# Attention and gated MLP, two layers, one token: output projection with the weights moving, and a new order of loads

## The chip, the cores and the metric

The kernel runs on one core of a Trainium2 chip. The metric is the time of one execution on the device in microseconds. Five runs of the kernel before gave 333.4 to 336.81, median 335.89.

## The reference

Four sequences (B), one new token each, model width 512. An attention block has 32 query heads of width 128 in 8 groups (four heads share one key and value head) and a cache of 4096 positions. Then comes a gated MLP of width 1792. Both blocks are applied twice, with the same weights and the same caches:

```
def _A_ref(x, k_cache, v_cache, wq, wo):
    q = (x @ wq).reshape(B, Sq, Hq, Dh) ...
    k = jnp.repeat(k_cache, rep, axis=1)
    v = jnp.repeat(v_cache, rep, axis=1)
    scores = jnp.einsum("bhqd,bhkd->bhqk", q, k) * (Dh ** -0.5)
    p = _softmax(scores, axis=-1)
    o = jnp.einsum("bhqk,bhkd->bhqd", p, v)
    return ... @ wo

def _B_ref(x, w_gate, w_up, w_down):
    h = _sigmoid(x @ w_gate) * (x @ w_up)
    return h @ w_down

x = x + _A_ref(_layernorm(x), k_cache, v_cache, wq, wo)
x = x + _B_ref(_layernorm(x), w_gate, w_up, w_down)
x = x + _A_ref(_layernorm(x), k_cache, v_cache, wq, wo)
x = x + _B_ref(_layernorm(x), w_gate, w_up, w_down)
```

Keys and values of a batch are each 8 groups x 4096 x 128 in bf16, 8 MiB; for four batches 32 MiB of keys and 32 MiB of values. They do not fit on the chip beside the weights, and layer 1 needs them again.

## The kernel before

**Tiles and slots.** A group's keys or values of one batch, 1 MiB, are loaded as two pieces of 512 KB (q = 0 and 1). A ring of 22 slots of one piece each (`NS`, `ring`) holds them; the weights have buffers of their own. Every load is issued by SyncE (SP), in the order that the string `order` spells (L413): a digit is a quarter of wq, a to d a quarter of wo, g, u, w the three MLP weights, k two K pieces (two groups, one q), V a V tile for layer 0, v a V tile for layer 1, r the K pieces of a batch that are loaded again. A load waits until the slot that it is given has no readers left. SP takes its queue strictly in order, so a load that waits for a slot holds up all loads behind it.

**What stays and what is loaded again.** V is loaded twice, once for each layer. K of a batch is loaded once, and its 16 pieces stay in the ring from layer 0's scores to layer 1's, but for those that `again` lists for the batch (L363, repeated at L414): these give their slot up after layer 0 and are loaded again by r.

**Work on one batch, layer 0.** VectorE transposes each K piece in place (`transpose_k`, L564). TensorE forms scores of a half of the groups (s = 0 or 1) in a bank S_ps, with q spread over a block-diagonal tile qbd as the stationary side and K moving, 16 matmuls of 512 columns for each q, each in a strip of 32 rows of the bank (`scores`, L577). `softmax` takes the maximum on VectorE, exponentials on ScalarE, and turns the probabilities with TensorE through the bank PT_ps into pt_sb. `values` multiplies V by them: narrow (L711), with V stationary, 32 matmuls of 4 columns for a group, or wide (`wide`, L673), with V moving, eight matmuls of 256 columns for a piece into the bank W_ps, which ScalarE copies into a bf16 high part (w_hi) and VectorE into a low part (w_lo), folded into O_ps by eight short matmuls. The tuple `NARROW` says which groups are narrow: in layer 0 all are, as in layer 1 those used before layer 0 of the next batch and those of the last batch; the other tiles of layer 1 are wide. VectorE scales O_ps into oT (L720). `y_proj` multiplies oT by wo: for each head four matmuls with wo stationary (128 x 128) and one column (four in layer 1) moving, all added up in the bank Y_ps over the 32 heads.

**From layer 0 to layer 1 (`cross`).** When the last V tile of a batch is used, `add_y` adds y to x, `glu` multiplies by wg and wu, `norm` makes the statistics (its matmuls go to the bank PT_ps), `centre` corrects for the mean on VectorE, `down` multiplies by wd, and `add_y` again gives layer 1's input. `q_proj` multiplies it by wq, `q_spread` makes qbd on TensorE and VectorE (L547), and layer 1's scores follow. Only when they are done do slots with K pieces come free. The last batch's layer 1 ends in `last_cross`, for all four batches at once.

**Order of instructions.** Nothing is ordered by hand within an engine. Each operation is put down with a duration, a priority (smaller is more urgent; steps of the cross have 0 or PX = 0), what it reads and writes; `_Sched.place` then plays the whole kernel through with these durations, a rate for the loads, a start-up charge after a pause (`RAMP`), and a time between blocks of TensorE's instructions (`FETCH`, `BLOCK`). Whenever an engine is free it takes, among the operations that could start within 0.05 us of the first, the most urgent. The order found so is written out, one in-order queue for each engine.

Of the kernel before, what the change touches and what calls it, by code (L numbers as in the profile page):

```python
# [6 lines left out]
ACTF = mybir.ActivationFunctionType  # L7
# [8 lines left out]
RAMP = 0.3  # L16
BLOCK = 256
FETCH = 5.7
PAIR = 0.0268
DRAIN = 0.13  # L20
# [21 lines left out]
class _Sched:  # L42
    def __init__(self, nslots):
        self.all = []
        self.last_write = {}
        self.readers = {}
        self.nslots = nslots
        self.bus = []

# [41 lines left out]
    def place(self):  # L91
# [18 lines left out]
        begun, crossed = 0, -FETCH  # L110
# [18 lines left out]
        while True:  # L129
            best = None  # L130
            for e in ENGINES:
# [3 lines left out]
                o = min((o for o in pending[e] if max(free_at[e], o.est) <= first + 0.05), key=lambda o: (o.prio, o.seq))  # L135
                t = max(free_at[e], o.est)
# [82 lines left out]
def bass_interleave_layers__gqa_block_cached__glu_gated_glu__decode_kernel(nc, A_x, A_k, A_v, A_wq, A_wo, B_x, B_wg, B_wu, B_wd, out):  # L219
# [22 lines left out]
    S = _Sched(NS)  # L242
    es = ExitStack()
# [66 lines left out]
    sel_o = sb("sel_o", [P, 2 * R], bf)  # L310

# [41 lines left out]
    S.put("pool", lambda e: e.memset(sel_o[:], 0.0), 0.1, 0, writes=["sel_o", "pl"])  # L353
    for a in range(4):
        S.put("pool", affine(sel_o, sel_o[:], [[-1, 2 * R]], -32 * a, 1.0), 0.2, 0, reads=["sel_o"], writes=["sel_o", "pl"])
    for name, t, v in (("ml0", ml, 1.0), ("S0", S_ps[0], 0.0), ("S1", S_ps[1], 0.0), ("S2", S_ps[2], 0.0), ("W", W_ps, 0.0)):
        S.put("dve", lambda e, t=t, v=v: e.memset(t[:], v), 0.4, 0, writes=[name])
# [5 lines left out]
    again = (((3, 1),), ((6, 1), (7, 0), (7, 1)), ((6, 1), (7, 1)), ((6, 0), (6, 1), (7, 0), (7, 1)))  # L363
# [49 lines left out]
    order = 'k10bkkkkk3Vk2VVkdVVcVagVVuwrvkkkkkkVvkkVVVVVVVvvkvvvkrkkkkvkvvVkVVVVVVVvvkvvvrkkkvvkvkkkVVVVVVVVrvvvvvvvvvvvvvv'  # L413
    again = (((3, 1),), ((6, 1), (7, 0), (7, 1)), ((6, 1), (7, 1)), ((6, 0), (6, 1), (7, 0), (7, 1)))  # L414
# [63 lines left out]
    def add_y(b, y, scal, skey, res, rkey, mi, prio):  # L478
# [4 lines left out]
            ), 0.2, prio, reads=["Y", rkey] + skey, writes=["xT"],  # L483
# [4 lines left out]
            ), 0.3, prio, reads=["Y", rkey] + skey, writes=["xj", "xsum0"],  # L488
# [45 lines left out]
    PS0, PS1, PL0, PL1, PV0, PV1, PK0, PK1, PDEN, PEV = (1.77, 1.93, -0.4, 1.55, 2.05, 1.65, 2.13, 2.82, 2.29, 1.1)  # L534
    cnt = {"u": 0}
    pt_free = list(range(NPT))
# [126 lines left out]
    def wide(l, b, s, pi, prio, gis):  # L663

        n = len(gis)
        for i, gi in enumerate(gis):
            for q in range(2):
                tile = V[l, b, 4 * s + gi, q]
                fns = []
                for j in range(HT // 2):  # L670
                    def fn(e, i=i, gi=gi, q=q, j=j, tile=tile):
                        a, t = j % 4, q * HT + 2 * j
                        return e.matmul(  # L673
                            W_ps[32 * a:32 * a + 2 * R, i * 256:i * 256 + 256],
# [5 lines left out]
                S.put("pe", fns, WIDE + DRAIN, prio, reads=[f"pt{pi}"], writes=["W"], tiles=[tile])  # L680
        w = 256 * n
        S.put(
            "act", lambda e: e.activation(w_hi[:, 0:w], W_ps[:, 0:w], ACTF.Copy), 0.62 if n > 1 else 0.4, PEV, reads=["W"],
# [3 lines left out]
            "dve", lambda e: e.tensor_tensor(w_lo[:, 0:w], W_ps[:, 0:w], w_hi[:, 0:w], ALU.subtract),  # L687
            0.65 if n > 1 else 0.4, PEV, reads=["W", "w_hi"], writes=["w_lo"],
# [10 lines left out]

    def values(l, b, s, pi, prio, gis, narrow):  # L700

        ws = [gi for gi in gis if gi not in narrow]
        for i in range(0, len(ws), 2):
            wide(l, b, s, pi, prio, ws[i:i + 2])
# [19 lines left out]
    def y_proj(l, s, prio, gis=range(4)):  # L724
        nb = 1 if l == 0 else B
        for gi in gis:
            fns = []
            for h in range(16 * s + gi * R, 16 * s + gi * R + R):
                for j in range(KD):
                    r = oT1[:, h:h + 1] if l == 0 else oT2[:, h, :]  # L730
                    fns.append(mm(
                        Y_ps[:, 0:nb * KD].rearrange("p (b k) -> p b k", b=nb)[:, :, j], wo[:, h, j * P:(j + 1) * P], r,
                        h == 0 and j == 0, h == H - 1 and j == KD - 1,
                    ))
# [236 lines left out]
```

## Time and profile before

| | |
|---|---|
| profiled execution, its own time | 335.89 us |
| its span, first to last instruction | 334.0 us |
| DMA, loads of SP: bytes, share of 16 engines | 119.82 MB, 93.9% |
| mean rate over the span | 361 GB/s |
| PE busy, matmuls | 208.6 us, 4968 |
| VectorE busy | 164.7 us |
| transposes of K pieces (L564) | 74, mean 1229 ns, 89.9 us |
| loads of K pieces / V pieces | 74 / 128, 512 KB each |
| projection by wo (Y_ps), layer 0 / layer 1 | 512 / 128 matmuls, mean 165 / 168 ns |
| copy of 512 columns to w_hi / subtraction to w_lo | mean 591 / 688 ns |

Busy times of matmuls overlap, so their mean is not the distance between two of them. Shares are means over the whole span; which resource ends last differs from stretch to stretch, so stretches are read apart. In the rows of stretches, the columns are: from and to in us, length, busy time (and count) of PE, its weight loads, VectorE, ScalarE, GpSimd, then the clock granted to TensorE, the share of the DMA engines, and GB/s. In rows of a timeline: start and duration in us, engine, line, operation, output <- inputs, shapes, and in brackets how long the engine idled before it and what ended that. The times at which single pieces land are the last of the 16 completions that the trace has for each load.

### The profile page before, as it was taken

What the parts mean: (1) busy time and instruction counts of PE and PEld (TensorE: products, weight loads), DVE (VectorE), ACT (ScalarE), POOL (GpSimd) and SP (SyncE); (2) the same over time, 40 slices, a digit from 0 to 9 for tenths busy, and PEclk for the clock granted to TensorE, in tenths of its full rate; (3) what the DMA queues carried; (4) which work ended last, traced back from release to release, by engine and by line L of the source; (5) the groups of instructions that cost most, each with busy time, mean ns of one, the idle gap of its engine ahead of it and who ended that gap; (6) DMA issues with size and microseconds to landing.
All of it is one profiled execution on the core that took longest, in us unless ns stands there. A gap on an engine that the chain in (4) does not pass through costs nothing.

```text
span 334.0 us, 11181 instructions
## 1 busy us (share of the span) xinstructions
PE 208.6 (62%) x4968; PEld 143.3 (43%) x4968; DVE 164.7 (49%) x418; ACT 62.3 (19%) x145; POOL 27.9 (8%) x111
## 2 busy tenths in 40 slices
PE   0224355444468677576865686868585766799864
PEld 0201323344433246454422455654142556565763
DVE  7088332002399781054996730348879404564013
ACT  1102013000014233000244221002154110105100
POOL 5201001000001111000000110000111000001101
PEclk9999999999995565555756555557555555567555
DMA  6999999999949999999999999987999999999930
GB/s 222 384 410 400 402 386 387 386 407 371 369 135 374 413 407 365 412 407 363 291 392 413 408 400 398 410 352 234 404 413 406 410 408 404 401 331 396 411 147 3
DMA packets 38337, 120.54 MB, mean 361 GB/s; under 512 B 3472, under 2 KB 9360, under 8 KB 38288
## 3 DMA queue, kind: packets, MB, share of 16 engines
q1 hardware_dynamic: 38256, 119.82, 93.9%
q8 instruction: 39, 0.64, 0.8%
q14 instruction: 10, 0.08, 0.1%
q10 hardware_dynamic: 32, 0.00, 0.0%
HBM read 119.80 MB, written 0.00 MB: 359 GB/s over the span
## 4 chain that ended last, share of the span: by engine, by line
DMA 50%; PE 18%; SPq 10%; issue 9%; DVE 8%; ACT 3%; POOLq 0%; POOL 0%; ACTq 0%; DVEq 0%
DMA ring<-in_A_v_cache_dram 32%; DMA ring<-in_A_k_cache_dram 18%; SPq L369 8%; PE S_ps L577 6%; DVE ring L564 3%; PE M_ps L326 3%; PE Y_ps L326 3%; PE W_ps L673 3%; PE O_ps L711 2%; ACT p_sb L618 2%; DVE ml L594 2%; SPq L390 2%; PE PT_ps L326 1%; ACT qbd L553 1%; DVE tr L611 0%
## 5 line engine op out<-in xcount | busy, mean ns | idle before, releaser
L564 DVE STREAM_TRANSPOSE ring<-ring 128x1024 int32<-128x1024 int32 x74 | 89.9, 1229 | 28.9 <-DMA ring<-in_A_k_cache_dram 28.4
L711 PE MATMUL O_ps<-pt_sb,ring 128*128 128x4 bf16 x1472 | 50.9, 167 | 34.4 <-DMA ring<-in_A_v_cache_dram 31.6
L577 PE MATMUL S_ps<-ring,qbd 128*16 128x512 bf16 x512 | 57.1, 598 | 19.6 <-DVE ring L564 12.3
L711 PEld LDWEIGHTS O_ps<-pt_sb,ring 128*128 128x128 bf16 x1472 | 45.4, 104 | 45.3 <-DMA ring<-in_A_v_cache_dram 32.6
L618 ACT ACTIVATE p_sb<-S_ps,cols 128x512 bf16<-128x512 f32 x32 | 24.6, 772 | 85.8 <-DVE cols L613 65.6
L577 PEld LDWEIGHTS S_ps<-ring,qbd 128*16 128x16 bf16 x512 | 14.2, 116 | 43.2 <-issue 25.1
L720 DVE TENSOR_TENSOR oT<-O_ps,winv 128x8 bf16<-128x8 f32 (+2 forms) x16 | 2.7, 166 | 59.3 <-PE O_ps L711 59.2
L594 DVE TENSOR_REDUCE ml<-S_ps 128x1 f32<-128x512 f32 x32 | 21.4, 668 | 13.2 <-PE S_ps L577 13.2
L673 PE MATMUL W_ps<-ring,pt_sb 128*8 128x256 bf16 x288 | 18.0, 381 | 8.5 <-DMA ring<-in_A_v_cache_dram 8.5
L326 PE MATMUL Y_ps<-oT,wo 128*128 128x1 bf16 x512 | 17.2, 165 | 6.4 <-DVE oT L720 3.6
L326 PEld LDWEIGHTS Y_ps<-oT,wo 128*128 128x128 bf16 x512 | 15.5, 104 | 7.9 <-DVE oT L720 4.4
L326 PE MATMUL PT_ps<-ident_b,p_sb 128*128 128x64 bf16 x128 | 12.4, 237 | 9.9 <-ACT p_sb L618 9.9
L326 PE MATMUL M_ps<-xT,wq 128*128 128x1 bf16 (+1 forms) x512 | 14.9, 164 | 4.7 <-issue 3.6
L326 PEld LDWEIGHTS M_ps<-xT,wq 128*128 128x128 bf16 x512 | 14.0, 100 | 8.2 <-issue 5.9
L460 POOL TENSOR_TENSOR cols<-cols 128x1 f32<-128x1 f32 (+1 forms) x10 | 6.6, 656 | 126.8 <-DVE cols L456 105.2
L643 POOL TENSOR_TENSOR cols<-cols 128x1 f32<-128x1 f32 x16 | 3.1, 193 | 158.8 <-ACT p_sb L618 158.8
L326 PEld LDWEIGHTS PT_ps<-ident_b,p_sb 128*128 128x128 bf16 x128 | 7.5, 119 | 17.4 <-ACT p_sb L618 13.8
L326 PE MATMUL Y_ps<-p_sb,wd 128*128 128x1 bf16 (+1 forms) x280 | 8.4, 166 | 10.3 <-DVE p_sb L754 6.3
L774 ACT ACTIVATE p_sb<-p_sb,cols 128x14 f32<-128x14 f32 x4 | 1.2, 307 | 68.1 <-DVE p_sb L518 47.1
L638 ACT ACTIVATE pt_sb<-PT_ps 128x512 bf16<-128x512 f32 x16 | 9.5, 596 | 20.6 <-PE PT_ps L326 20.6
L626 ACT ACTIVATE p_sb<-PT_ps 128x512 bf16<-128x512 f32 x16 | 9.5, 596 | 20.2 <-PE PT_ps L326 17.8
L326 PEld LDWEIGHTS Y_ps<-p_sb,wd 128*128 128x128 bf16 x280 | 7.9, 104 | 11.9 <-DVE p_sb L754 7.8
(118 smaller groups left out, 205.5 us busy)
## 6 DMA issues: line engine op xcount, KB each, us to landing
ring<-in_A_v_cache_dram SPq DMA_DIRECT2D x128, 512.0 KB, 10.8
ring<-in_A_k_cache_dram SPq DMA_DIRECT2D x74, 512.0 KB, 11.1
wq<-in_A_wq_dram SPq DMA_DIRECT2D x4, 1024.0 KB, 12.5
wo<-in_A_wo_dram SPq DMA_DIRECT2D x4, 1024.0 KB, 12.7
wg<-in_B_w_gate_dram SPq DMA_DIRECT2D x1, 1792.0 KB, 15.6
wu<-in_B_w_up_dram SPq DMA_DIRECT2D x1, 1792.0 KB, 17.2
wd<-in_B_w_down_dram SPq DMA_DIRECT2D x1, 1792.0 KB, 21.9
w_hi<-in_A_x_dram SPq DMA_DIRECT2D x1, 4.0 KB, 1.7
```

The lines of the kernel that those rows point to most:

```text
L326: return lambda e: e.matmul(o, lhsT=l, rhs=r, start=start, stop=stop)
L369: return e.dma_start(ring[t.slot], t.src.rearrange("(p t) d -> p (t d)", p=P)[:, q * TS:(q + 1) * TS])
L390: S.put("sp", lambda e: e.dma_start(o, i), 0.43, 0, writes=[key], dma=key, nbytes=nbytes, rate=rate)
L460: "pool", lambda e: e.tensor_tensor(rs, vpe[:, 0:nb], mhalf[:, 0:nb], ALU.pow), 0.6, prio,
L564: return e.transpose(v, v)
L577: return e.matmul(bank[32 * gi:32 * gi + 16, :], lhsT=qbd[u % NQB][:, gi, nn, :], rhs=kt[:, :, nn // 2, :, nn % 2], start=nn == 0, stop=nn ...
L594: "dve", lambda e, q=q: e.tensor_reduce(ml[:, q:q + 1], S_ps[banks[q]][:], AX.X, ALU.max, negate=True), 0.65,
L618: "act", lambda e, q=q: e.activation(p_sb[:, 4 * q:4 * q + 4, :].rearrange("p c x -> p (c x)"), S_ps[banks[q]][:], ACTF.Exp, bias=nbias, s ...
L626: "act", lambda e: e.activation(pt1.rearrange("p c g a h -> p (c g a h)"), PT_ps[:], ACTF.Copy), 0.65, prio,
L638: "act", lambda e: e.activation(pt_sb[pi][:].rearrange("p c g t h -> p (c g t h)"), PT_ps[:], ACTF.Copy), 0.65,
L673: return e.matmul(W_ps[32 * a:32 * a + 2 * R, i * 256:i * 256 + 256], lhsT=pt_sb[pi][:, t // 4, gi, t % 4:t % 4 + 2, :].rearrange("p t h - ...
L711: return e.matmul(O_ps[:, gi * R:(gi + 1) * R], lhsT=ring[tile.slot][:, (t % HT) * DH:(t % HT + 1) * DH], rhs=pt_sb[pi][:, t // 4, gi, t % ...
```

## The change

`y_proj` has wo as the moving side for groups 0 to 6: each of the four heads of a group takes a strip of 32 rows of Y_ps (one row used, four in layer 1), with oT as the stationary side and 512 columns of wo moving; the strips add up over the groups. After group 6 the bank is split into a high and a low part (w_hi by ScalarE, w_lo by VectorE), and eight matmuls with the new selector `sel_y` sum the strips and turn them into columns in PT_ps. Group 7, the last tile, is added there the old way. y, the up product of `glu` and `down` therefore live in PT_ps, no longer in Y_ps, and the statistics move to whichever scores bank is idle (`spare`). `wide` takes its bank as an argument. Group ranges in which layer 0 uses V follow `parts` (three groups, then one, for both halves). The planner gets new constants and a `look`: on VectorE an urgent operation that becomes ready within 0.7 us is preferred to one that could start now. The order of loads and the list of reloads are new; K pieces loaded again go from 1, 3, 2, 4 to 1, 0, 0, 3 for batches 0 to 3.

```diff
-RAMP = 0.3
+RAMP = 0.4
-FETCH = 5.7
+FETCH = 6.1
...
-        begun, crossed = 0, -FETCH
+        begun, crossed = 63, -FETCH
...
                 o = min((o for o in pending[e] if max(free_at[e], o.est) <= first + 0.05), key=lambda o: (o.prio, o.seq))
+                near = [
+                    p for p in pending[e]
+                    if p.prio <= 0 < o.prio and max(free_at[e], p.est) <= first + min(self.look.get(e, 0.0), o.dur)
+                ]
+                if near:
+                    o = min(near, key=lambda p: (p.est, p.seq))
...
+    S.look = dict(zip(("dve", "pe", "act"), (0.7, 0.0, 0.0)))
...
+    sel_y = sb("sel_y", [P, B], bf)
...
-    again = (((3, 1),), ((6, 1), (7, 0), (7, 1)), ((6, 1), (7, 1)), ((6, 0), (6, 1), (7, 0), (7, 1)))
+    again = (((7, 1),), (), (), ((5, 1), (6, 1), (7, 1)))
...
-    order = 'k10bkkkkk3Vk2VVkdVVcVagVVuwrvkkkkkkVvkkVVVVVVVvvkvvvkrkkkkvkvvVkVVVVVVVvvkvvvrkkkvvkvkkkVVVVVVVVrvvvvvvvvvvvvvv'
+    order = 'bk1kkk0dkV2kVkV3kVVVcVagVuwrvkkkkkvkkvkVvVVVVVVVvkvkvkrkvkkvvkkVVVVVVVVvvvrvkkkkkvkvkvvkVVVVVVVVvvvvvvrvvvvvvvv'
...
-    PS0, PS1, PL0, PL1, PV0, PV1, PK0, PK1, PDEN, PEV = (1.77, 1.93, -0.4, 1.55, 2.05, 1.65, 2.13, 2.82, 2.29, 1.1)
+    PS0, PS1, PL0, PL1, PV0, PV1, PK0, PK1, PDEN, PEV = (1.77, 2.41, -0.4, 1.76, 2.04, 1.65, 1.02, 2.04, 0.59, 1.1)
...
+    def spare():
+
+        i = (2 * cnt["u"] + 2) % 3
+        return S_ps[i], f"S{i}"
...
-    def y_proj(l, s, prio, gis=range(4)):
+    def y_proj(l, s, prio, gis):
...
+            if g < G - 1:
+                fns = [
+                    mm(Y_ps[32 * a:32 * a + nb, :], of(g * R + a), wo[:, g * R + a, :], g == 0, g == G - 2) for a in range(R)
+                ]
+                S.put("pe", fns, 0.43 + DRAIN, prio, reads=keys, writes=["Y"])
+            else:
+                fns = []
+                for h in range(g * R, g * R + R):
+                    for j in range(KD):
+                        fns.append(mm(y[:, :, j], wo[:, h, j * P:(j + 1) * P], of(h), False, h == H - 1 and j == KD - 1))
+                S.put("pe", fns, 0, prio, reads=keys, writes=["PT"])
+            if g == G - 2:
+                S.put("act", lambda e: e.activation(w_hi[:], Y_ps[:], ACTF.Copy), 0.62, prio, reads=["Y"], writes=["w_hi"])
+                S.put(
+                    "dve", lambda e: e.tensor_tensor(w_lo[:], Y_ps[:], w_hi[:], ALU.subtract), 0.65, prio,
+                    reads=["Y", "w_hi"], writes=["w_lo"],
+                )
+                fns = []
                 for j in range(KD):
+                    for x, half in enumerate((w_hi, w_lo)):
+                        fns.append(mm(y[:, :, j], half[:, j * P:(j + 1) * P], sel_y[:, 0:nb], j == 0 and x == 0, False))
+                S.put("pe", fns, 0, prio, reads=["w_hi", "w_lo", "sel_y"], writes=["PT"])
...
-        g, u = glu(n, lambda k: xT[:, k, 0:n], "xT", lambda: norm(b, 0, 4.0, rs, "rs_h", PT_ps, "PT", prio), prio)
+        g, u = glu(n, lambda k: xT[:, k, 0:n], "xT", lambda: norm(b, 0, 4.0, rs, "rs_h", *spare(), prio), prio)
...
+    def parts(narrow):
+
+        if len(narrow) == 4:
+            return range(0, 3), range(3, 4)
+        if 3 in narrow:
+            return range(0, 2), range(2, 3), range(3, 4)
+        return range(0, 2), range(2, 4)
```

## The prediction

> **What bounds the kernel now.** I read the page's slices first, then busy time by stretches, then the chain that ended last in order of time, then the timeline of VectorE in one stretch.
>
> ```profile
> span 334.0 us, 11181 instructions
> PE 208.6 (62%) x4968; PEld 143.3 (43%) x4968; DVE 164.7 (49%) x418; ACT 62.3 (19%) x145; POOL 27.9 (8%) x111
> ...
> DMA  6999999999949999999999999987999999999930
> ...
> q1 hardware_dynamic: 38256, 119.82, 93.9%
> q8 instruction: 39, 0.64, 0.8%
> ```
>
> No engine is near full; the loads are. Where the DMA row shows less than 9 there are a start, a tail, and holes in between: one for each batch, when layer 1's queries of that batch are being made (I call these turns 0 to 3). In stretches (the last two columns are DMA share and GB/s):
>
> ```profile
> 88.00:92.00 4.00, 0.86 (x23) 0.77 (x23) 1.16 (x7) 0.00 (x0) 0.31 (x1) 1.00 0.79 313
> 92.00:96.00 4.00, 2.81 (x32) 0.97 (x32) 4.00 (x6) 0.00 (x0) 0.25 (x1) 1.00 0.01 2
> ...
> 156.00:160.00 4.00, 1.58 (x16) 0.55 (x20) 3.19 (x4) 0.23 (x1) 0.00 (x0) 0.50 0.95 294
> ...
> 224.00:228.00 4.00, 3.24 (x50) 1.58 (x54) 2.44 (x8) 0.60 (x1) 0.55 (x1) 0.50 0.55 190
> 228.00:232.00 4.00, 4.00 (x108) 2.62 (x104) 3.79 (x8) 0.00 (x0) 0.00 (x0) 0.84 0.73 208
> ```
>
> Between turns the loads run at 405 to 407 GB/s (180 to 220 us, 240 to 292 us), which is 1.29 us for a piece of 512 KB, and the trace has them land 1.28 us apart. Against 407 GB/s the turns lose 6.8 us (88 to 104: 16 minus 4 x (313+2+257+365)/407), 2.9 (156 to 168), 4.6 (224 to 236) and 1.1 (296 to 300). So the time is bytes plus holes plus a tail of 11.7 us after the last landing at 322.3.
>
> Why there are holes: of the 22 ring slots, K pieces of the batch stay in place for layer 1 until its first scores have read them. Turn 1: the last layer-0 V piece of batch 1 landed at 140.28; the first K slots came free when the first scores ended, 160.35, or 20.1 us later; a load issued then landed at 165.30, 4.95 us on. What those 20 us contain:
>
> ```profile
> 147.86 0.19 DVE L518 SCALAR_TENSOR_TENSOR p_sb<-csum_wg,cols,M_ps 128x14 f32<-128x14 f32 x1
> 147.97 1.24 DVE L564 STREAM_TRANSPOSE ring<-ring 128x1024 int32<-128x1024 int32 x1
> 149.13 0.19 DVE L518 SCALAR_TENSOR_TENSOR p_sb<-csum_wu,cols,Y_ps 128x14 f32<-128x14 f32 x1
> ...
> 156.81 1.25 DVE L564 STREAM_TRANSPOSE ring<-ring 128x1024 int32<-128x1024 int32 x1 [1.73 <-DMA ring<-in_A_k_cache_dram]
> 157.98 0.39 DVE L547 TENSOR_TENSOR qbd<-M_ps,mask_a 128x256 bf16<-128x256 f32 x1
> ```
>
> VectorE works in order. A K transpose (1.24 us) stands ahead of the gate's next step, and at 156.81 one that waits for a load stands ahead of qbd, ready at 155.7: 2.2 us of chain.
>
> **The change, part by part.** *Reloads.* K pieces that are loaded a second time go from 1, 3, 2, 4 (batches 0 to 3) to 1, 0, 0, 3: six pieces, 3.146 MB. By the row (407 GB/s) that is 7.7 us. The Trainium skill ("DMA: Bandwidth & Descriptors", Specifications) limits HBM to about 358 GB/s for a core, which would make it 8.8; the measured stretch decides, **-7.7 us**. Six transposes of 1.23 us leave VectorE too. But those pieces now keep their slots: slots left free in the turns go from 7, 9, 8, 10 to 7, 6, 6, 9. A reload costs 1.28 us of load and its slot hides 1.28 us of hole, so while a turn has a hole, dropping a reload alone is worth nothing. The gain must come from shorter turns or from turns with cover to spare. That needs turn by turn working.
>
> *Turn 0.* Both orders have loaded 29.25 MiB when the last weight, wd, is in; it lands at 83.9 either way, and the free slots are 7 either way. The chain from there to free slots was 11.3 us (83.87 to 95.20). VectorE transposes hold up xT (ready about 85.7, starts 86.34) and qbd (ready 92.1, starts 92.83): 1.4 us. The planner's new `look` prefers an urgent step within 0.7 us to starting such a transpose; I count half, **-0.7**. An instruction stall of 2.09 us at 87.99 may move either way (-2 to +1); I take 0.
>
> *Turn 1.* Before, 17 pieces could land between the last V piece and the first load that needed a released slot. Now the order gives v, K, v, K, v, K (tiles of two pieces), 12 pieces, after which it is blocked. First blocked piece: release + 4.5 (between the 4.44 of turn 0 and the 4.95 of turn 1), the thirteenth, due at 13 x 1.28 = 16.6 us. With the old chain of 20.1 the hole is 8.0 us; before it was 2.2 to the same point (late landings at 161.27 and 165.30: 0.7 + 1.5). The chain should shorten, though: the transpose that waited ahead of qbd was caused by late K pieces, and these now land at 9 and 10 us after the V, before qbd (-2.2); the earlier pair lands 2.6 us sooner, and with `look` I take 1.0 of the 1.7 us it cost. At 16.9 us the hole is 4.8. **+2.6**, between +5.8 (old chain) and 0.
>
> *Turn 2.* Chain 19.2 us (209.50 to 228.71), of which 3.3 is again VectorE: it waited 2.30 us for a K landing and transposed twice, with the gate's steps behind. Cover falls from 16 pieces to 14 (v, v, v, v, K, K, K). With a chain of 17 the fifteenth would be 2.3 late, but its slots also hang on the wide products of older V tiles, which before freed theirs only at 11.7 and 15.7 us after the V; that gives about 3.8 against 4.8 before (landings at 228.98, 232.75, 234.60). **-1.0**, between +0.3 and -3.
>
> *Turn 3.* The three reloads now stand behind six V tiles of batch 2, where four stood ahead of them; the queue was short of slots there (lags of 4.3 to 6.7 us from issue to landing around 294). **-1.0**, between 0 and -1.1, the whole hole.
>
> *Output projection.* For seven of eight groups, 16 matmuls of one column (27 ns apart, 0.43 us) become four of 512 columns in four column strips. Nearest row: S_ps L577, also strips of 512 columns; groups of four start 427 ns apart. The skill speaks against the gain ("TensorEngine Tiling (Array Packing)", Key Properties): changing the tiling mode drains the array. The trace agrees: after the last strip of scores a full-array matmul starts 561 ns later (median; 320 at the full clock) where neighbours of one mode are 27 ns apart, and entry costs 95. A lone group then costs 0.66 us against 0.46; a run of three 1.5 against 1.3. Without the drain it would be a tie. So PE loses 0.2 us a group, which hides in waits for V (35 waits, 31.6 us) except at a turn.
>
> *The fold.* Copy on ACT (w_hi row, 0.59), subtraction on VectorE (w_lo row, 0.69), 8 matmuls (0.22): 1.7 us with hand-overs, five times. It runs beside the last V tile, whose second piece lands 1.28 us after its first, and its own path (product 0.6, oT 0.3, 16 matmuls 0.6, 1.5 us: 209.50 to 210.99) is about as long. If the strips end 0.1 us before that landing, the fold ends near +1.7: 0.2 late. Turn 0 hides it behind wd; turns 1 to 3 and the tail pay, **+0.8**. Behind the fold's matmuls PE queues the last tile's projection and the gate; if placed badly, up to 1.3 us each time (ACT plus VectorE exposed); if well, 0.
>
> *Instructions.* Seven groups lose 24 each (matmuls and weight loads), the fold adds 16: 152 fewer, five times, 760 of 9936, about three of the 39 code blocks on q8. In busy stretches those fetches follow 6.2 us apart (131.98, 137.93, 144.13, 150.36), and PE stands still when it outruns them: 2.1, 0.5, 1.5, 1.1 us in the four turns. Inside a turn only 16 net instructions go, so I count nothing, -1 to +1 in all.
>
> *At no cost:* the memset of Y and five more GpSimd fills (0.49 us, about 1 us) run before the first weights land; without that cover 0.5. Statistics in a scores bank that is idle: same instructions, and the transposes' bank is left free for y; if its reader were late, 0.2 a turn. The wide product's second bank is not reached in layer 0, whose groups are all narrow. Layer-0 groups taken three and one in both halves: the oT of group 1 comes a tile later, covered by V loads. Issues on SP per piece stay; in the first stage wq0 comes at 7 MiB in place of 3, so first scores start near 25 us, not 20; slots needed by the V tiles behind them stay free in time (first needed about 44, freed about 35).
>
> Sum: -7.7 - 0.7 + 2.6 - 1.0 - 1.0 + 0.8 = **-7.0**. The profiled execution took 335.89 (span 334.0 and 1.9 around it), which is also the median of the runs shown. 335.9 - 7.0 = **328.9 us**.
>
> **Rivals.** *A: the holes take it back.* Chains stay as long as they were (other transposes or code stalls take the place of those removed): turn 1 +5.8, turns 0, 2, 3 nothing, fold +0.8: -1.1, 334.8 us. For it: VectorE stays 45% busy and in order. Against: the waiting transpose had a cause that goes.
> *B: turns shrink fully.* Turn 1 without VectorE and ordering losses is near 15 us: +0.7 in place of +2.6, turn 2 -2.5, turn 0 -1.4: 324.8 us, say 325. Against: a chain that short runs into the 6.2 us of code fetches.
> *C: slower, by starved V loads.* In batches 1 and 2, 16 slots are now held while layer 0's V streams through six: a round is 6 x 1.28 = 7.7 us and needs 4.5 from issue to landing, so a piece may stay 3.2 us. Before, V pieces of batch 1 stayed up to 3.1 (landed 122.30, slot reissued 125.38) while softmax filled PE, later ones 0.7. Each us of excess x costs 5.3 x (32 pieces in rounds of six). It decides from x = 1.6 on, eating 7.0 + 1.7; at 1.8 the time is 338.4. Against: V of those groups now comes four tiles after the last K, 15 us, where about 10 are needed.
>
> **How the numbers follow.** The runs of before spread 1%; about 0.5% (1.7 us) can be told from no change. Likeliest 0.50 (326 to 332.5), A 0.22 (332.5 to 337), B 0.15 (324 to 326), C 0.13. Faster (under 334.2): 0.50 + 0.15 + a third of A, 0.72; same (334.2 to 337.6): the rest of A, 0.15; slower: C, 0.13. Range: 325 leaves out about half of B; 337.5 leaves out C.
>
> **What would show it.** Right: 68 K loads in place of 74, 116.7 MB on q1; turn 1's hole about 2 us larger and turn 2's smaller; no transpose that waits for a load ahead of qbd there; PE near 4590 matmuls. Rival A: time from last V to first released slot still 19 to 20 us in turns 1 and 2. C: the DMA row below 9 between turns. The prediction falls if turn 1's hole exceeds 9 us, or if the fold's VectorE step stands behind a transpose every time.

## The result, and the profile after

The changed kernel took 332.23 us (median of 25 runs, 330.5 to 334.91), the kernel before 334.52 (median of 46 runs beside it, 332.36 to 338.16): ratio 0.9937, 95% interval 0.9917 to 0.9958. So it is faster, by 2.3 us, where 7.0 were predicted; 332.2 lies above 328.9, inside the wide range, and inside the likeliest case's own range of 326 to 332.5 only by a hair. The two profiled executions are 3.7 us apart (335.89 and 332.22), because the one of before lay 1.4 us above its group's median; the accounting below is of these two.

The clock granted to TensorE is no rival explanation: it was lower in the changed kernel (0.58 to 0.71 as a mean over an execution, 0.68 to 0.72 before), but the changed kernel's executions at 0.65 and over were only 0.5 us faster in the median than those below, and in turns 1 to 3 both profiles have rows of 0.50.

The page of the changed kernel:

```profile
span 330.3 us, 10482 instructions
PE 212.0 (64%) x4612; PEld 132.8 (40%) x4612; DVE 161.6 (49%) x416; ACT 65.4 (20%) x149; POOL 28.8 (9%) x116
...
DMA  6999999999979999997799999979999999999900
...
q1 hardware_dynamic: 37392, 116.67, 92.8%
q8 instruction: 36, 0.59, 0.7%
```

The counts are those forecast: 116.67 MB on q1 (3.15 less), 36 code blocks on q8 (three less), 4612 matmuls against some 4590 (two more V tiles of layer 1 are narrow). But the share of q1 fell from 93.9% to 92.8%: fewer bytes, and more time between them. The last piece landed 5.7 us earlier (316.58 against 322.26), and the tail after it grew by 2.0 us, to 13.74. In stretches, the columns as before:

```profile
88.00:92.00 4.00, 1.86 (x20) 0.70 (x24) 3.79 (x8) 0.00 (x0) 0.56 (x1) 0.50 0.78 309
92.00:96.00 4.00, 3.43 (x84) 2.08 (x76) 3.83 (x9) 0.00 (x0) 0.00 (x0) 0.84 0.67 152
...
152.00:156.00 4.00, 2.87 (x96) 2.71 (x96) 3.68 (x11) 0.42 (x1) 0.00 (x0) 0.50 0.79 256
156.00:160.00 4.00, 3.48 (x73) 1.76 (x73) 1.53 (x7) 0.00 (x0) 0.55 (x1) 0.50 0.39 101
...
220.00:224.00 4.00, 3.40 (x94) 2.51 (x95) 3.60 (x10) 0.60 (x1) 0.55 (x1) 0.50 0.49 165
```

Turn 0's hole (92 to 96) has filled from 2 GB/s to 152; turn 1 now has a hole of 101 GB/s at 156 to 160, where 294 GB/s stood; turn 2's has only moved. VectorE in turn 1:

```profile
150.51 1.24 DVE L575 STREAM_TRANSPOSE ring<-ring 128x1024 int32<-128x1024 int32 x1
151.68 0.18 DVE L528 SCALAR_TENSOR_TENSOR p_sb<-csum_wu,cols,PT_ps 128x14 f32<-128x14 f32 x1
...
152.28 2.50 DVE L575 STREAM_TRANSPOSE ring<-ring 128x1024 int32<-128x1024 int32 x2 [0.21 <-DMA ring<-in_A_k_cache_dram]
154.70 0.18 DVE L491 SCALAR_TENSOR_TENSOR xT<-PT_ps,cols,xj 128x4 bf16<-128x4 f32 x1
...
158.32 0.42 DVE L558 TENSOR_TENSOR qbd<-M_ps,mask_a 128x256 bf16<-128x256 f32 x1 [0.50 <-PE M_ps L335]
```

The transpose that stood ahead of qbd is gone, as forecast; qbd now waits for PE. Two transposes stand ahead of the second xT instead and hold it up by about 0.5 us (its last product was done at 154.15).

For the sum I take the time between landings beyond 1.28 us for each piece, by stretch: a turn runs from the last layer-0 V piece of a batch (turn 0: from wd) to the first of the next batch (turn 3: to the last load), V from there on. The fold's 0.8 is spread over the four places that were to pay it. The last three columns are experiments told below: five reloads put back, 21 slots, strips put together.

| us | predicted change | before | after | reloads back | 21 slots | strips together |
|---|---|---|---|---|---|---|
| six pieces, 7.7 us of bytes | -7.7 | | -7.7 | | | |
| turn 0 | -0.7 | 7.75 | 4.68 | 4.23 | 6.06 | 4.57 |
| V of batch 1 | 0 | 1.29 | 2.53 | -0.03 | 4.87 | 2.64 |
| turn 1 | +2.8 | 3.93 | 7.14 | 4.78 | 10.18 | 6.57 |
| V of batch 2 | 0 | 0.01 | 0.77 | 0.20 | 0.91 | 1.26 |
| turn 2 | -0.8 | 5.66 | 5.85 | 4.55 | 6.96 | 6.03 |
| V of batch 3 | 0 | -0.01 | 0.12 | 0.18 | 2.74 | 0.10 |
| turn 3 | -0.8 | 2.14 | 1.88 | 2.14 | 3.03 | 1.48 |
| tail | +0.2 | 11.75 | 13.74 | 13.83 | 13.77 | 12.52 |

From before to after the rows add up to -3.5; the other 0.2 lies before wd.

### The profile page after: what moved, and what is told of

Read it like the earlier page. It is cut to its first block, busy times and chain, and to the rows that moved or that the text cites. A ratio compares the mean times of both kernels' runs of the same rounds, so it can differ in the third digit from the quotient of the medians.

```text
span 330.3 us, 10482 instructions
## 1 busy us (share of the span) xinstructions
PE 212.0 (64%) x4612; PEld 132.8 (40%) x4612; DVE 161.6 (49%) x416; ACT 65.4 (20%) x149; POOL 28.8 (9%) x116
## 3 DMA queue, kind: packets, MB, share of 16 engines
q1 hardware_dynamic: 37392, 116.67, 92.8%
## 4 chain that ended last, share of the span: by engine, by line
DMA 55%; PE 18%; DVE 12%; issue 7%; ACT 4%; SPq 3%; POOLq 0%; POOL 0%; ACTq 0%; DVEq 0%
DMA ring<-in_A_v_cache_dram 38%; DMA ring<-in_A_k_cache_dram 11%; PE S_ps L588 7%; DVE ring L575 6%; DMA wq<-in_A_wq_dram 5%; PE O_ps L728 4%; PE PT_ps L335 3%; ACT p_sb L629 3%; PE M_ps L335 2%; SPq L379 2%; DVE ml L605 2%; PE W_ps L684 1%; ACT qbd L564 1%; PE Y_ps L335 1%; ACT pt_sb L649 1%
## 5 line engine op out<-in xcount | busy, mean ns | idle before, releaser
L575 DVE STREAM_TRANSPOSE ring<-ring 128x1024 int32<-128x1024 int32 x68 | 83.3, 1235 | 27.9 <-DMA ring<-in_A_k_cache_dram 27.3
L728 PE MATMUL O_ps<-pt_sb,ring 128*128 128x4 bf16 x1536 | 52.8, 167 | 36.1 <-DMA ring<-in_A_v_cache_dram 32.7
L728 PEld LDWEIGHTS O_ps<-pt_sb,ring 128*128 128x128 bf16 x1536 | 46.9, 104 | 56.1 <-DMA ring<-in_A_v_cache_dram 39.0
L737 DVE TENSOR_TENSOR oT<-O_ps,winv 128x12 bf16<-128x12 f32 (+1 forms) x16 | 2.6, 166 | 57.3 <-PE O_ps L728 57.3
L684 PE MATMUL W_ps<-ring,pt_sb 128*8 128x256 bf16 x256 | 16.5, 375 | 4.8 <-DMA ring<-in_A_v_cache_dram 4.8
L335 PE MATMUL Y_ps<-wo,oT 128*1 128x512 bf16 x112 | 15.6, 601 | 2.5 <-DVE oT L737 1.4
L335 PE MATMUL M_ps<-xTj,wq 128*128 128x4 bf16 x128 | 3.7, 166 | 19.8 <-DMA wq<-in_A_wq_dram 19.8
L335 PEld LDWEIGHTS PT_ps<-ident_b,p_sb 128*128 128x128 bf16 x128 | 7.2, 116 | 16.3 <-ACT p_sb L629 15.1
L335 PE MATMUL PT_ps<-p_sb,wd 128*128 128x1 bf16 (+1 forms) x280 | 8.6, 166 | 8.1 <-DMA wd<-in_B_w_down_dram 3.6
L764 ACT ACTIVATE w_hi<-Y_ps 128x512 bf16<-128x512 f32 x5 | 3.0, 597 | 50.8 <-PE Y_ps L335 50.8
L335 PEld LDWEIGHTS PT_ps<-p_sb,wd 128*128 128x128 bf16 x280 | 8.0, 104 | 9.8 <-issue 5.2
## 6 DMA issues: line engine op xcount, KB each, us to landing
ring<-in_A_k_cache_dram SPq DMA_DIRECT2D x68, 512.0 KB, 10.1
```

What stands on the lines that cost most here:

```text
L335: return lambda e: e.matmul(o, lhsT=l, rhs=r, start=start, stop=stop)
L575: return e.transpose(v, v)
L684: return e.matmul(bank[32 * a:32 * a + 2 * R, i * 256:i * 256 + 256], lhsT=pt_sb[pi][:, t // 4, gi, t % 4:t % 4 + 2, :].rearrange("p t h - ...
L728: return e.matmul(O_ps[:, gi * R:(gi + 1) * R], lhsT=ring[tile.slot][:, (t % HT) * DH:(t % HT + 1) * DH], rhs=pt_sb[pi][:, t // 4, gi, t % ...
```

## The experiments

Every time is a median beside runs of the kernel before on the same chip; ratios are against that kernel, with 95% intervals. Each edit also lets the planner place everything anew, so the order of instructions differs in more than the edit, and small differences may come from that. In the texts on record, F is the theory that the fold on the path sets the time, S that ring slots do, and later letters are explained where they stand.

### What the dropped reloads are worth

The kernel before, with no reloads in batches 1 and 2 and nothing else changed:

```diff
-again = (((3, 1),), ((6, 1), (7, 0), (7, 1)), ((6, 1), (7, 1)), ((6, 0), ...
+again = (((3, 1),), (), (), ((6, 0), ...
```

> The kernel before with no reloads of K in batches 1 and 2 (five pieces less, 2.6 MB), its order of loads, projection and planner untouched. Theory S, a reload costs 1.28 us of load and its slot hides 1.28 us of hole: bytes -6.4, holes of turns 1 and 2 +6.4 in all: 334.5, within 1.5. Rival bytes: the holes stay as they are and the time falls to about 328. Rival C, V starved in six slots: besides the holes the V stretches of batches 1 and 2 show landings more than 1.28 us apart, together 2 us or more, and the time is 336 or over.

Measured: 337.13 us, 1.0077 (1.0045 to 1.0108), slower, with 2.6 MB less to load. Its profiled execution was its fastest (333.71), so I take only directions from it: turn 1 lost 1.6 us, turn 2 1.0, and V of batches 1 and 2 lost 1.3 and 1.2. That is rival C of the text above (336 or over, 2 us or more in the V stretches). The 2.6 us are not the slots' alone: PE's long idles put to issue, which the section on instructions in a turn explains, also grew in this execution, from 5.6 to 12.0 us.

The changed kernel with those five reloads put back:

```diff
-again = (((7, 1),), (), (), ((5, 1), (6, 1), (7, 1)))
+again = (((7, 1),), ((6, 1), (7, 0), (7, 1)), ((6, 1), (7, 1)), ((5, 1), (6, 1), (7, 1)))
```

> The changed kernel with the five reloads of batches 1 and 2 put back where its order has their place (in batch 1 behind the third pair of K, in batch 2 behind the third V tile). The kernel before without these reloads was 0.8% slower, not faster. Theory S with starved V loads: 2.6 MB more are 6.4 us of loads, the holes of turns 1 and 2 shrink by 5 to 6 us, and the V stretches get back the 2 us that they lost: 330 to 332.5 us. Rival bytes: holes as they are, 338.

Measured: 332.83 us, 0.9949 (0.9908 to 0.999), no different from the changed kernel's 0.9937: a hair above what theory S expected, and far from rival bytes (338). Three stretches of the changed kernel:

```profile
116.00:134.00 18.00, 11.50 (x250) 7.19 (x248) 5.76 (x15) 4.02 (x8) 1.25 (x6) 0.50 0.96 355
...
146.00:166.00 20.00, 15.82 (x412) 11.04 (x412) 13.51 (x43) 1.37 (x3) 1.12 (x2) 0.59 0.81 277
216.00:234.00 18.00, 14.93 (x318) 9.27 (x322) 15.01 (x34) 3.27 (x7) 1.49 (x5) 0.50 0.84 298
```

and the same stretches with the reloads back:

```profile
116.00:134.00 18.00, 12.40 (x276) 8.11 (x277) 5.61 (x15) 3.57 (x8) 0.93 (x4) 0.50 1.03 409
...
146.00:166.00 20.00, 15.55 (x355) 9.78 (x355) 17.31 (x42) 3.13 (x7) 2.06 (x6) 0.59 0.92 330
216.00:234.00 18.00, 14.54 (x274) 8.18 (x274) 16.21 (x36) 3.42 (x7) 1.49 (x5) 0.50 0.91 324
```

The last column is all there is to see: 54, 53 and 26 GB/s more over 18, 20 and 18 us are 0.97, 1.06 and 0.47 MB, together 2.5 of the 2.6 MB that came back. The reloads run entirely in time that is otherwise empty. By the table, their five pieces cost 6.4 us and the stretches of batches 1 and 2 give 6.8 back (2.6, 2.4, 0.6, 1.3, less 0.1 of rounding): 3.7 in the turns, 3.1 in V.

The changed kernel with one slot less (`NS = 21`):

> The changed kernel with 21 slots in the ring instead of 22. Theory S (slots bind in the turns and for V of batches 1 and 2): one piece less of cover in each of four turns, 4 x 1.28 = 5.1 us, and in batches 1 and 2 V goes round in five slots, 6.4 us, of which 4.5 from issue to landing; the starved stretches then lose 1 to 3 us each more. In all 337.5 to 343, ratio 1.016 to 1.032. Rival (code supply alone sets the turns, and slots come early enough): under 334, ratio below 1.003.

Measured: 342.99 us, 1.0239 (1.0195 to 1.0283): 10.8 us for one slot of 22 by the medians, 10.1 by the ratios.

```profile
116.00:134.00 18.00, 10.24 (x224) 6.46 (x216) 6.08 (x16) 4.02 (x8) 0.93 (x4) 0.50 0.92 331
134.00:146.00 12.00, 6.89 (x152) 4.51 (x149) 0.33 (x2) 0.00 (x0) 0.00 (x0) 0.50 0.96 351
146.00:166.00 20.00, 16.23 (x395) 10.43 (x395) 10.95 (x36) 1.50 (x3) 1.11 (x2) 0.52 0.70 261
```

The V stretch 134 to 146, which ran at 414 GB/s with 22 slots, runs at 351. The chains of the turns did not move (from the last V landing to the first score 16.47, 15.66, 16.08 and 16.11 us, against 16.47, 15.44, 16.30 and 16.08); what grew is the time between landings, so this is slots. Theory S holds, at the upper end of what it expected, though V of batch 2 lost only 0.1 us more and V of batch 3, of which it said nothing, 2.6.

### What the fold costs

The old projection for all groups, in Y_ps, no fold; the rest stays changed:

```diff
+            if True:
+                yo = Y_ps[:, 0:nb * KD].rearrange("p (b k) -> p b k", b=nb)
+                ... mm(yo[:, :, j], wo[:, h, j * P:(j + 1) * P], of(h), h == 0 and j == 0, ...)
+                continue
             if g < G - 1:
```

> The changed kernel with the projection of before (16 matmuls of one column for every group, added up in Y_ps, no strips and no fold); loads, reloads and planner as in the changed kernel. Theory F, the fold is on the path: in the changed kernel the step from the last V piece's landing to xT takes 3.98, 3.97 and 3.99 us in turns 1 to 3 and 3.52 in the tail, against 2.47, 1.52, 2.47 and 1.53 before. Without the fold the tail loses 2.0 us and turns 1 to 3 become 1.5 to 2.5 us shorter, of which the holes of turns 1 and 2 pass on most: 332.2 - 2.0 - 1.5 - 2.0 - 0.5, about 326 us. Rival I, fewer instructions are the gain: 760 PE instructions return, code fetches stall the turns again, 333 to 335 us. Rival H, only the slots set the turns: within 1 us of 332.2, but for the tail.

Measured: 337.3 us, 1.0089 (1.0059 to 1.0119). F (326) falls; I has the direction and not the size. xT did come earlier, 1.52 us after the last V piece in turns 1 to 3 in place of 3.97, and in turn 1 qbd followed (14.30 for 14.96), but in turns 2 and 3 qbd came at 17.65 and 18.17 in place of 15.82 and 15.60. In turn 2:

```profile
213.84 0.17 DVE L800 SCALAR_TENSOR_TENSOR p_sb<-p_sb 128x14 bf16<-128x14 f32 x1
215.30 0.53 PEld L684 LDWEIGHTS W_ps<-ring,pt_sb 128*8 128x8 bf16 x16 [2.10 <-issue]
215.30 1.03 PE L684 MATMUL W_ps<-ring,pt_sb 128*8 128x256 bf16 x16 [2.02 <-issue]
```

The input of `down` is ready at about 214.0, and PE starts only at 215.30; "issue" says that it waited for nothing that the profile shows. What it waited for is told in the section on instructions in a turn.

The same in layer 1 alone, where the fold stands only in the tail:

> The changed kernel with the projection of before in layer 1 alone (once, ahead of the end). Theory F: only the tail changes, from 13.7 us after the last landing to about 11.7, so 330.2 us. Rival I: 152 instructions return in the last stage, where the loads end the wait: no more than 0.3 us slower than theory F says. If the tail has grown for another cause (the statistics in a scores bank, y in PT_ps): 332.2.

Measured: 332.35 us, 0.9927 (0.9899 to 0.9956), as the changed kernel; F's time is not met. xTj came at 2.32 instead of 3.52, after an idle of 0.85 us put to issue inside the projection, and in this execution the write of the output took 3.09 us from issue to end, 1.78 in the changed kernel, so its tail was 13.85. Whether the five runs beside it had that slow write is not known; without it this execution would have been 1.3 us shorter.

Strips for groups 0 to 3 only, the fold after group 3:

```diff
-            if g < G - 1:
+            if g < 4:
...
-            if g == G - 2:
+            if g == 3:
```

> The changed kernel with strips for groups 0 to 3 only: the fold comes after group 3, with four V tiles (10 us of loads) still to come, and groups 4 to 7 are added the old way. Theory F: the fold is hidden, the step from last V landing to xT is back near 1.5 to 2.5 us, time near that of the old projection, about 326 us, and if instructions matter (380 fewer than there would be) up to 1 us less. Rival I: 332 to 334. Rival H: within 1 us of 332.2 but for the tail.

Measured: 334.89 us, 1.0008 (0.9975 to 1.004). The tail fell to 12.05 and xT stood at 1.52 in every turn, but turns 2 and 3 lost 7.5 and 3.6 us (5.9 and 1.9 in the changed kernel), with PE idles of 1.5, 1.6 and 1.8 us (from 212.1, 279.9, 285.9) without a wait. None of the three theories has this time; I (332 to 334) is nearest.

The last attempt of this kind puts the reloads back and folds after group 5 in layer 1 alone:

> The changed kernel with the five reloads of batches 1 and 2 put back (that alone measured 332.8), and in layer 1 alone the fold after group 5, with groups 6 and 7 projected the old way. Aim: a version better than both. If the fold on the path is what makes the tail 2 us longer: xTj 1.6 us after the last landing in place of 3.5, tail 12, time 331, ratio 0.988. If code supply fills the gap as it did with the old projection in layer 1: tail 13 to 14, time 332.5 to 333.5, ratio 0.993 to 0.996.

Measured: 333.29 us, 0.996 (0.9929 to 0.9992). That is the second of the two cases expected, but not for its reason: no idle put to issue stands in this tail. xTj still came at 3.25, since the oT of groups 4 to 6 comes as one instruction after group 6's products, a V product stands between the two strips that follow, and two groups are projected the old way behind the fold.

All these take the fold off the path by adding instructions. Where the fold's time goes in the changed kernel can be read in the tail (last landing at 316.58; start and duration first):

```profile
316.11 0.60 PE L335 MATMUL Y_ps<-wo,q1T 128*4 128x512 bf16 x4
316.64 0.50 PEld L728 LDWEIGHTS O_ps<-pt_sb,ring 128*128 128x128 bf16 x16 [0.44 <-DMA ring<-in_A_v_cache_dram]
316.64 0.59 PE L728 MATMUL O_ps<-pt_sb,ring 128*128 128x4 bf16 x16
...
317.16 0.60 PE L335 MATMUL Y_ps<-wo,q1T 128*4 128x512 bf16 x4
...
317.81 0.60 ACT L764 ACTIVATE w_hi<-Y_ps 128x512 bf16<-128x512 f32 x1 [7.08 <-PE Y_ps L335]
318.44 0.69 DVE L766 TENSOR_TENSOR w_lo<-Y_ps,w_hi 128x512 bf16<-128x512 f32 x1 [1.00 <-ACT w_hi L764]
...
319.28 0.17 PE L335 MATMUL PT_ps<-sel_y,w_hi 128*128 128x4 bf16 x1 [1.52 <-DVE w_lo L766]
...
320.10 0.17 DVE L824 TENSOR_TENSOR xTj<-PT_ps,xj 128x16 bf16<-128x16 f32 x1 [0.97 <-PE PT_ps L335]
```

The oT of groups 4 to 6 is ready together, at 315.0. But their strips are three steps that write one bank, and the planner put the two pieces of the last V tile between them: in its book a step that writes the bank of the step before can start only 0.13 us (`DRAIN`) after PE comes free, and a less urgent product that could start at once was taken. So the copy starts 1.23 us after the last landing, not before it, and everything behind it is on the path. This suggests an edit without more instructions: the strips of one call as one step.

```diff
+        row = [4 * s + gi for gi in gis if 4 * s + gi < G - 1]
...
+            if g < G - 1 and g < row[-1]:
+                continue
...
-                    mm(Y_ps[32 * a:32 * a + nb, :], of(g * R + a), wo[:, g * R + a, :], g == 0, g == G - 2) for a in range(R)
+                    mm(Y_ps[32 * a:32 * a + nb, :], of(x * R + a), wo[:, x * R + a, :], x == 0, x == G - 2) for x in row for a in range(R)
```

> The changed kernel with the same instructions, but the strips of the groups that come in one call put down as one step of 12 (or 8) matmuls, so that in PE's queue they all stand ahead of the last V tile's products. Theory Q (the fold is late because of its place in the queue): the fold's copy starts about 0.1 us after the last landing and not 1.2 after it, xT comes 2.4 to 2.9 us after the landing in place of 3.97, xTj 2.3 in place of 3.5, the tail is 12.5; the turns keep what they gain, since the number of instructions is the same: 4 x 1.1 = 4.4 us, 328 us, ratio 0.980. Rival D (PE's code supply fills whatever the fold leaves in the turns): only the tail gains, 1.2 us, 331, ratio 0.990. Rival L (the copies themselves are the lateness): xT still at +3.5 or more, 332.

Measured: **330.07 us, 0.9868 (0.9825 to 0.991)**, better than both kernels. The same place:

```profile
314.57 1.45 PE L335 MATMUL Y_ps<-wo,q1T 128*4 128x512 bf16 x12 [0.34 <-DVE q1T L737]
...
315.96 1.01 PE L728 MATMUL O_ps<-pt_sb,ring 128*128 128x4 bf16 x32
316.08 0.60 ACT L768 ACTIVATE w_hi<-Y_ps 128x512 bf16<-128x512 f32 x1 [5.22 <-PE Y_ps L335]
316.71 0.69 DVE L770 TENSOR_TENSOR w_lo<-Y_ps,w_hi 128x512 bf16<-128x512 f32 x1 [2.19 <-ACT w_hi L768]
...
317.54 0.17 PE L335 MATMUL PT_ps<-sel_y,w_hi 128*128 128x4 bf16 x1 [0.57 <-DVE q1T L737]
...
317.75 0.57 PE L335 MATMUL PT_ps<-q1T,wo 128*128 128x4 bf16 x16
318.36 0.17 DVE L828 TENSOR_TENSOR xTj<-PT_ps,xj 128x16 bf16<-128x16 f32 x1 [0.89 <-PE PT_ps L335]
```

The copy starts with the last landing (316.07), xTj comes 2.29 after it, and the tail is 12.52, 1.22 shorter. In turns 1 to 3 xT comes 1.28 us earlier, and yet turns and V stretches together gain only about 0.3 us. Turns 2 and 3 show where it went. In turn 2 the second xT was 1.1 us earlier and qbd was no earlier at all:

```profile
220.08 1.25 DVE L575 STREAM_TRANSPOSE ring<-ring 128x1024 int32<-128x1024 int32 x1 [2.73 <-DMA ring<-in_A_k_cache_dram]
221.25 0.12 DVE L511 COPY cols<-S_ps 128x1 f32<-128x1 f32 x1
...
222.05 1.24 DVE L575 STREAM_TRANSPOSE ring<-ring 128x1024 int32<-128x1024 int32 x1
223.22 0.38 DVE L558 TENSOR_TENSOR qbd<-M_ps,mask_a 128x256 bf16<-128x256 f32 x1
```

PE gave qbd's input at 222.47; a transpose held VectorE until 223.2, and another had held up the statistics at 221.25. In turn 3 the products with wd stop before the last three; these ran in the changed kernel at

```profile
286.12 0.22 PE L335 MATMUL PT_ps<-p_sb,wd 128*128 128x1 bf16 x3 [1.22 <-issue]
```

and with the strips together at

```profile
285.83 0.24 PE L335 MATMUL PT_ps<-p_sb,wd 128*128 128x1 bf16 x3 [2.01 <-issue]
```

Counted from the last V piece, PE began these products 1.0 us earlier and idled 0.8 us longer before the last three. In turn 1 such an idle, 0.59 us, is new and takes half of the gain. So the lateness is the place in PE's queue (theory Q) and not the copies, and it was worth its time in the tail alone; in the turns other things end last, as rival D said: VectorE in turn 2, PE's supply of code in turn 3. The time lies between Q's 328 and D's 331, nearer to D's.

With the five reloads back as well:

> The same with the five reloads of batches 1 and 2 put back, which alone were worth nothing (332.8). If reloads and turns add up: the time of e12 within 1 us. With shorter turns there is less hole for the reloads to be loaded in, so if Q holds this should be up to 2 us slower than e12 (330); if D holds, equal (331).

Measured: 331.04 us, 0.989 (0.9867 to 0.9913); the interval meets that of the version without reloads. Again they are worth nothing either way.

### What instructions in a turn cost

Two kernels add the same PE time after the up and gate products of each turn, once as 64 matmuls of one column (128 instructions with their weight loads), once as four of 512 columns (8 instructions). The products go to Y_ps, which is idle then, and nobody reads them; the rest is computed as before.

```diff
+S.put("pe", [mm(Y_ps[:, 0:1], wg[:, 0, 0:P], xT[:, 0, 0:1]) for _ in range(64)], 0, ...)        # 64 short
+S.put("pe", [mm(Y_ps[:], wg[:, 0, 0:P], wg[:, 1, 0:512]) for _ in range(4)], 1.72 + DRAIN, ...)  # 4 long
```

> The changed kernel with 64 extra matmuls of one column in each turn, behind the gate's and up's products, into the idle Y_ps; their result is not used. 128 instructions more, 64 x 27 ns = 1.7 us of PE. With the old projection put back the turns came out no shorter although xT was 2.45 us earlier, so the new theory is I: a turn is as long as its PE code takes to be fetched, 6.2 us for 256 instructions. Theory I: 128 x 6.2 / 256 = 3.1 us longer in each of turns 1 to 3, and most of it shows in the holes: 332.2 + 5 to 9, so 337 to 341 us. Theory F (busy time and hand-overs on the path set the turn): 1.7 us in each, 335 to 337. Turn 0 waits for wd meanwhile and hides it in both.

> The same place with the same PE time in few instructions: four extra matmuls of 512 columns, 4 x 427 ns = 1.7 us, 8 instructions; result not used. Theory I: 0.2 us of code a turn, and the PE time goes into waits for code that are there anyway: 332 to 334 us, well below the 64 short ones. Theory F: the same as the 64 short ones, 335 to 337.

Measured: 347.01 us, 1.0358 (1.0313 to 1.0402) for the short ones; 338.02, 1.0095 (1.0061 to 1.0129) for the long ones. Turn 1 with the short ones:

```profile
153.18 0.33 PE L335 MATMUL Y_ps<-xT,wg 128*128 128x1 bf16 x7
154.78 1.68 PE L335 MATMUL Y_ps<-xT,wg 128*128 128x1 bf16 x57 [1.27 <-issue]
```

and with the long ones:

```profile
152.23 1.87 PE L335 MATMUL Y_ps<-wg 128*128 128x512 bf16 x4
```

PE is busy about as long, but the short ones are cut by an idle of 1.27 us put to issue. First scores come 18.8, 19.9, 17.9 and 21.0 us after the last V piece with the short ones, 16.6, 15.4, 16.0 and 16.1 with the long ones (16.5, 15.4, 16.3 and 16.1 without either). The difference is 9.0 us, 2.2 a turn for 120 instructions; at the 6.2 us between code blocks of 256 that the prediction read from q8, 120 instructions would be 2.9. But 6.2 us is not a least distance: in every trace some two blocks begin 3.4 to 4.0 us apart.

That these idles are waits for code can be read from the traces. In the 16 traces of this case PE idles for over 0.4 us with the idle put to issue 74 times. Of these idles 70 end 2.2 to 2.8 us after the DMA packet of a code block on q8 began; of 1293 idles as long that ended with a known wait, 6% do. (The other four are the 4.7 us near 35 us in kernels with the old order of loads.) After wd has landed such idles are 2.5 us in the changed kernel, 8.3 with the short matmuls, 0.4 with the long ones, and 11.3 with the old projection, whose input of `down` above waited so: a block began at 212.82, and PE went on at 215.30.

Theory I has the difference, then, and neither of the two levels; F has nearly the level of the long ones and not that the two differ. The long ones are not free: their 1.87 us of PE time in each turn cost 5.8 us in all (5.3 by the ratios), although scores come no later; in turn 1 wide products are done later, and with them the slots that the next loads wait for (v0.6's two pieces issued at 154.67 and 156.78, in the changed kernel at 151.33 and 151.76).

### Which part carries the gain

The changed projection, statistics and group ranges with the loads, reloads, priorities and planner of before:

> The new projection alone (strips, fold, y in PT_ps, statistics in the scores bank, three groups then one) with loads, reloads, priorities and planner of before. Theory I: the projection's 760 instructions fewer are the change's gain, as the old projection in the changed kernel cost 5 us: 334.5 - 4 to 5, so 329.5 to 331. Rival: what was gained by it was gained only with the order and planner made for it: 334 or over. Theory F: slower than before, 336.

Measured: 338.06 us, 1.0105 (1.0052 to 1.0159). The rival holds (334 or over). Turn 0 is already shorter (5.19), turn 3 longer (5.00), and the tail is 13.82.

The kernel before with the new planner alone, and the changed kernel with the old planner (`RAMP` 0.3, `FETCH` 5.7, `begun` 0, no `look`):

> The kernel before with nothing changed but the planner: its constants for the start-up charge and the code blocks (0.4, 6.1, first block 63 further on) and the preference of 0.7 us on VectorE. Projection, loads, reloads and priorities are those of before. Theory P (the gain of the change lies in the order of instructions; the profiled turn 0 was 3.1 us shorter): about 331.5, ratio 0.991, hole of turn 0 near 5, no transpose ahead of xT and qbd in the turns. Theory O (the parts pay only together: the projection alone was 1.05% slower, the rest alone 0.9% slower): 334.5 to 337, ratio 1.000 to 1.007, since 0.7 us for an urgent step saves at most 0.5 us a turn while the code blocks fall elsewhere.

> The changed kernel with the planner of before (its three constants, no preference on VectorE); projection, loads, reloads and priorities stay changed. Theory P: the gain goes, 334.5 to 336, ratio about 1.00, turn 0 back to a hole of 7 to 8 us. Theory O: anything that moves the code blocks away from where the order was searched costs, 334 to 338, but turn 0 keeps its shorter hole (about 5), as it did with the projection alone. If 332 to 333 comes out, the planner is worth nothing and the load order alone carries the gain.

Measured: 333.81 us, 0.9965 (0.9937 to 0.9994), and 336.15 us, 1.0054 (1.0027 to 1.0081). The planner is worth 3.9 us in the changed kernel; by itself it is worth 1.2 us by the ratio and 0.6 by the medians, hardly clear of nothing. In turn 1 of the changed kernel without it, a transpose of 1.25 us stands ahead of xT, which comes at 5.85. Neither P (331.5) nor O (334.5 or more) has the first number; it lies between. The second is O's, in time and in turn 0. Turn 0 keeps its short hole without the planner (4.96), and also without the projection (5.31 with the old one), so no single part of these owns that gain.

## Why the prediction was right and wrong

**Reloads, -7.7: the step that failed.** The bytes went as counted; what failed is what was set against them. The prediction wrote that dropping a reload alone is worth nothing while a turn has a hole, and then let turn 1 alone pay for the slots kept (+2.6), with turns 2 and 3 shorter and the V stretches at nothing. Put back in the changed kernel, five of the six reloads change nothing (332.83 for 332.23): their 6.4 us of loads give 6.8 back, and 3.1 of these lie in the V stretches. Taken out of the kernel before, they cost 2.6 us. The size was missed in two places. V of batches 1 to 3 was rival C's mechanism, given the threshold x = 1.6 and a chance of 0.13 as an alternative; it came at once and small, +2.1 us in all (V of batch 1 ran short at 122.3, where a load waited for a slot whose own piece had landed at 121.6). It should have stood in the sum as a term, not as a rival. And turn 2, -1.0, had the chain fall to 17 us; the scores ended 18.2 after the last V piece, with an idle of 1.3 us for code from 218.5 and two transposes behind it. With turn 3 (-0.3 for -1.0) that is 1.5 us missed.

**Turn 1, +2.6: right in sign and near in size, but for the cover.** The chain was taken at 16.9 us and took 17.3. The thirteenth piece did hang on the first scores, as forecast: it was issued at 160.77 and landed 5.6 us on where 4.5 was taken, 6.3 us late for 4.8. But the queue had stopped two pieces before it. The slot of the eleventh hung on a wide product of v0.6, whose piece had landed on time, at 154.89, but which PE came to only at 157.00, behind `q_proj`; the eleventh was issued at 157.64 and came 4.9 us late. Over the whole turn the loss was 3.2.

**Turn 0, -0.7: right sign, too small.** -3.1. The idle of 2.09 us within `q_proj`, which was given "-2 to +1" and taken as 0, is gone, and the transpose ahead of xT too. Where a code block falls was not worked out, so this gain was luck. The products with wq in the kernel before:

```profile
86.58 1.41 PE L326 MATMUL M_ps<-xT,wq 128*128 128x2 bf16 x47 [0.95 <-DVE xT L481]
90.09 0.61 PE L326 MATMUL M_ps<-xT,wq 128*128 128x2 bf16 x17 [2.09 <-issue]
```

and in the changed one:

```profile
85.76 1.87 PE L335 MATMUL M_ps<-xT,wq 128*128 128x2 bf16 x64 [0.32 <-DVE xT L491]
```

**The fold, +0.8: the second step that failed.** It rested on the words "if the strips end 0.1 us before that landing". They ended 1.2 after it, since PE took the last V tile between them: 2.0 us in the tail for 0.2, and 1.5 to 2.45 in the turns. Moving the strips alone gave 1.22 of the tail back. The other 0.8 stays: the last group's sixteen matmuls (317.75, 0.57 us) stand behind the fold's, while the sum let the fold end at +1.7 beside them and gave that queue only as a range. The switch between modes that the Trainium skill names ("TensorEngine Tiling (Array Packing)", Key Properties) is small here. A group's four strips hold PE for 0.53 us until the next V product (316.11 to 316.64), three groups together for 1.38 (314.57 to 315.96), 0.46 each: about 0.1 for a change. The rule and the sum's 0.2 a group, hidden, were not what failed; the order of the groups was.

**Instructions, nothing: mis-sized.** The old projection in the changed kernel is 5 us slower (337.3), and 120 instructions in each turn cost 9. Of the 152 in each projection the prediction counted the 16 inside a turn and left out those ahead of it, which move the places where PE waits for code. In the profiled pair these waits in the four turns went from the 2.1, 0.5, 1.5 and 1.1 us that the prediction read to 0, 0, 1.3 and 1.2, 2.6 us less (2.1 of them in turn 0); with the old projection in the changed kernel they and the later ones are 11.3 us.

**Sum.** With the fold spread as in the table: turn 0 -2.4 against the forecast, turn 1 +0.4, turn 2 +1.0, turn 3 +0.5, V +2.1, tail +1.8, before wd -0.2: +3.2, which takes -7.0 to -3.8; the profiled pair shows -3.7. The chances (0.72 for faster) were on the right side. Rival A, the holes take it back, gave 334.8; it had the mechanism, but neither the gain of turn 0 nor the loss in the tail.

What stays open is which loads or priorities of the new plan make 1.05% slower (projection alone) and 0.9% slower (the changed kernel without it) into 0.6% faster together. The planner accounts for 3.9 us of it; the order of loads and the priorities were not tried apart.

## What to carry to other kernels

When a load is dropped and its data keep the buffer, count the buffer and not the bytes: by this kernel's slots, five pieces saved were worth nothing and one slot lost cost 10 to 11 us. Look at the order in which a planner can put a step that has been cut into pieces: steps that write one bank leave room between them, and the work that slips in there may be what the step had to be ahead of. And an edit that takes short instructions out of a critical stretch may be worth more than its busy time.

## What the hardware showed that was not expected

- The same PE time as 128 instructions or as 8 in a turn made 9.0 us of difference over four turns. PE's long idles put to issue end 2.2 to 2.8 us after a code block on q8 began to load, 70 of 74 times.
- One slot of 512 KB out of 22 was worth 3.0 to 3.2% of the time, while the turns' chains stayed within 0.25 us.
- The write of a 4 KB output took 3.09 us from issue to the end of the span in one of the 16 profiled executions and about 1.8 in the others.
